# A fifth head pair whose softmax weights TensorE transposes in the banks of their own scores, with the first queries on another queue and a new list of schedule numbers

## The chip, the cores and the metric

One core of one Trainium2 chip runs the whole program. The metric is device time in microseconds of one launch, the median of several. A profile of one execution goes with it.

## The reference

Attention over a batch of 4, 8 heads, 576 tokens and 64 dimensions a head, then two feed-forward layers over the 2304 tokens, all in float32:

```python
scores = (q @ k.T) / sqrt(64)
scores = where(scores >= max(scores) - tau, scores, -1e9)      # tau = 0.02, by row
attn = exp(scores - max); attn = attn / (sum(attn) + 1e-9)
x = (attn @ v) as (2304, 512)
x = relu(x @ w1_in) ** 2 @ w1_out        # 512 -> 2048 -> 512
x = max(0.01 * h, h) @ w2_out            # h = x @ w2_in
```

## The kernel before

**Work and steps.** Heads are taken in pairs, so that there are 16 pairs (4 per batch element), numbered here from 0: the fifth pair is pair 4, the first of the second batch element. A pair has nine steps, each a block of 128 rows of scores: eight of 128 queries of one head, and one of the 64 remaining queries of both heads. A step multiplies queries and keys into two PSUM banks `s` (L498), takes the negated row maximum `nb` on VectorE (L508), the exponential `e` on ScalarE (L509), the threshold `th` and the masked product with its row sum on VectorE (L513), and the reciprocal `r` (L518). The ring `s` has two members, so step k+2 may write only when all that reads step k's banks is done.

**Two ways from there.** For pairs 0 to 3 (`nav=4`), `e` is scaled by `r` in float32 (L522 to L524), TensorE transposes it block by block into `pt` (L532, L533; two banks of a pool `ps_t` of their own, ring of one), ScalarE copies that into `PT`, and five float32 products with the values give an output chunk `o` (L598). For pairs 4 to 15 the weights are split into two float16 parts (`P16`; ScalarE L523 or another engine, and VectorE L554), a DMA transposes them into `PT` (L560), and fifteen float16 products give `o` (L594). Pairs 0 to 5 (`nat`) have float32 queries and keys, the later ones split them too. An output chunk leaves by ScalarE (`tmp`, L606), a sum into `xs` (ScalarE L608 and GpSimd L609, or VectorE L611) and a DMA into `x1d`.

**The feed-forward work.** Twelve of the 16 blocks of the first layer run for the first 1792 tokens in pieces (`h` L642, `y0`/`y1` L666) between the attention steps from the fifth pair on: their banks, `psf`, are opened when `ps_t` is closed, and their input is the first batch element's output. The rest of both layers (L775, L821) follows alone. Each weight block is read as float64 (`wraw`) and made into float32 and two parts by ScalarE and VectorE (L341 to L346), GpSimd and others; twelve blocks of the first layer are made beside the first pairs.

**Order.** Nothing is ordered by hand. `Plan.order` takes all operations with their priorities (`prio`, mostly the step number plus a number of `CFG`), models the time of each, and writes one fixed order per engine, choosing between engines by `price`. So each number of `CFG` can move any instruction. DMAs are issued by SyncE (SP), the first few by ScalarE's queue: `tau`, the first weight block's two halves, the first pair's queries, and `eye`.

Of the kernel before, what the change touches and what calls it, by code (L numbers as in the profile page):

```python
# [7 lines left out]
F32 = mybir.dt.float32  # L8
# [15 lines left out]

CFG = dict(
    price=[{'V': 4.8, 'A': 1.81, 'G': 1.1},
           {'V': 3.0, 'A': 0.84, 'G': 1.01},
           {'V': 2.82, 'A': 1.42, 'G': 1.25},
           {'V': 1.99, 'A': 1.06, 'G': 1.2},
           {'V': 3.0, 'A': 2.4, 'G': 1.5}],  # L30
    lead1=-2.0, xsg0=[0, 1, 2, 3], lbm=8, lb=[[0, 4], [0], [5], [0, 1, 2, 3, 5, 6]], xsm=4, xsg=[0, 3], dq=1.15,
    xu=False, pqk=-2.996, pd1=-0.75, pex=-1.791, pd2=0.3, ph=2.017, pl=1.4, hu=False, bg=2.008, lead=2.5, w0=22.155,
    wstep=2.3, fend=1.0, tol=0.2, hor=-0.021, xlead=5.801, nb=3, eb=3, pb=3, ptb=3, kvb=3, nat=(0, 1, 2, 3, 4, 5),
    nav=4, vb=2, tmb=1, gb=2, xb=1, w2step=2.57, wo=0.316, wrb=3, r1b=1, xrb=1,
)


# [208 lines left out]
def tile_kernel(ctx: ExitStack, tc: tile.TileContext, qT, kT, vv, w1, w2, tau, eye, out):  # L246
# [151 lines left out]
    def times(o, n):  # L398
# [1 line left out]
        return [("V", dve(n, True, True), lambda: nc.vector.tensor_scalar(out=o(), in0=o(), scalar1=qsc, scalar2=None, op0=ALU.mult), "K"),  # L400
                ("A", act(n, ap=True), lambda: nc.scalar.activation(o(), o(), AF.Copy, scale=qsc), "K"),
                ("G", pool1(n, True), lambda: nc.gpsimd.tensor_scalar(out=o(), in0=o(), scalar1=qsc, scalar2=1.0, op0=ALU.mult, op1=ALU.mult), "K")]
    order = [(b, p) for b in range(B) for p in range(NP)]
    steps = [(n, h, t) for n in range(len(order)) for h, t in
             [(0, 0), (0, 1), (1, 0), (1, 1), (0, 2), (0, 3), (None, MAIN), (1, 2), (1, 3)]]
    NS = len(steps)
    SPP = NS // len(order)
    SPB = SPP * NP

    def prep(n):  # L410
        b, p = order[n]
        o = pairs[n] = Box()
        h0 = 2 * p
# [46 lines left out]
        if n < CFG["nav"]:  # L460
# [15 lines left out]
    def step(i):  # L476
# [48 lines left out]
        if n < CFG["nav"]:  # L525

            op(scale(ev), [e, r_], [e], i + CFG["ph"], CFG["hu"])
            pt = val("ps_t", "pt", 1, [P, NH, P], F32)

            def flip():  # L530
                for j in range(MAIN):
                    nc.tensor.transpose(pt.get()[:, j], ev()[:, REM + j * P:REM + (j + 1) * P], eye_sb)  # L532
                nc.tensor.transpose(pt.get()[:, MAIN], ev()[:, 0:P], eye_sb)  # L533
            op(("T", NH * 0.109, flip), [e, eye_v], [pt], i + CFG["pl"], True)
            for dst, col, c0, c1 in ([(chunk(n, hh, 1), 2 * P, hh * REM, (hh + 1) * REM) for hh in range(2)] if h is None
                                     else [(chunk(n, h, t // 2), t % 2 * P, 0, P)]):
                op(rnd(lambda dst=dst, col=col, c0=c0, c1=c1: whole32(dst)[:, :, col:col + c1 - c0], lambda c0=c0, c1=c1: pt.get()[:, :, c0:c1], NH * (c1 - c0), True),
                   [pt], [dst], i + CFG["pl"], True)
# [33 lines left out]

    def values(key, i):
        n, h, c = key
        b, p = order[n]
        o = pairs[n]
        t0, w = spans[c]
        pt = chunks[key]
        pr = i + (CFG["lead1"] if n % NP == NP - 1 else CFG["lead"])
        ps = val("ps_o", "o", 1, [P, 512], F32)  # L580


# [24 lines left out]
        if key[0] % CFG["xsm"] in CFG["xsg0" if key[0] < NP else "xsg"]:  # L607
# [295 lines left out]
```

## Time and profile before

| | us |
|---|---|
| median of 3 runs | 1135.37 (1129.83 to 1136.39) |
| the profiled execution | 1133.95 |
| its span, first to last instruction | 1132.2 |
| TensorE busy in it | 1070.7 |
| VectorE / ScalarE / GpSimd busy | 689.3 / 544.4 / 596.4 |

The profile is of one execution. "Busy" is the union of an engine's recorded instructions; an idle time before an instruction is put down to what ended last before it started. The launch costs 1.75 us beside the span.

### The profile page before, as it was taken

What the parts mean: (1) busy time and instruction counts of PE and PEld (TensorE: products, weight loads), DVE (VectorE), ACT (ScalarE), POOL (GpSimd) and SP (SyncE); (2) the same over time, 40 slices, a digit from 0 to 9 for tenths busy, and PEclk for the clock granted to TensorE, in tenths of its full rate; (3) what the DMA queues carried; (4) which work ended last, traced back from release to release, by engine and by line L of the source; (5) the groups of instructions that cost most, each with busy time, mean ns of one, the idle gap of its engine ahead of it and who ended that gap; (6) DMA issues with size and microseconds to landing.
All of it is one profiled execution on the core that took longest, in us unless ns stands there. A gap on an engine that the chain in (4) does not pass through costs nothing.

```text
span 1132.2 us, 17792 instructions
## 1 busy us (share of the span) xinstructions
PE 1070.7 (95%) x6308; PEld 883.8 (78%) x6308; DVE 689.3 (61%) x1316; ACT 544.4 (48%) x978; POOL 596.4 (53%) x626
## 2 busy tenths in 40 slices
PE   5888799899999999999999999999999999999998
PEld 3544488688889988899888778878888888888887
DVE  4888998789878888864879985571312221211122
ACT  3887878778877788865434452231211111111121
POOL 3667678678776787654656664442322322232222
PEclk9999999999999999999999999999999999999999
DMA  5344578998998796865444365430010010010010
GB/s 151 104 133 119 147 164 174 180 163 171 176 160 166 148 169 116 152 107 174 151 153 131 112 199 173 158 121 1 28 48 1 1 56 1 1 38 1 0 39 19
DMA packets 197673, 121.83 MB, mean 108 GB/s; under 512 B 156752, under 2 KB 175312, under 8 KB 197584
## 3 DMA queue, kind: packets, MB, share of 16 engines
q1 hardware_dynamic: 196848, 119.28, 44.9%
q10 hardware_dynamic: 736, 1.41, 0.4%
q8 instruction: 50, 0.82, 0.3%
q14 instruction: 39, 0.32, 0.1%
HBM read 70.98 MB, written 17.83 MB: 78 GB/s over the span
## 4 chain that ended last, share of the span: by engine, by line
PE 71%; DVE 6%; DMA 5%; issue 3%; ACT 3%; POOL 2%; SPq 0%; POOLq 0%; DVEq 0%; ACTq 0%
PE y L821 23%; PE h L775 22%; PE y L666 8%; PE h L642 7%; PE o L594 5%; PE s L498 5%; DMA PT<-P 4%; DVE wraw L344 2%; DVE wraw L346 1%; ACT e L509 1%; DVE e L513 1%; DVE nb L508 1%; DVE wraw L342 1%; POOL gl L298 0%; PE o L598 0%
## 5 line engine op out<-in xcount | busy, mean ns | idle before, releaser
L298 POOL TENSOR_TENSOR gl<-r,gh 128x512 fp32r<-128x512 f32 (+1 forms) x140 | 182.0, 1301 | 323.6 <-DVE gh L287 272.8
L787 DVE TENSOR_TENSOR r<-h,r 128x512 f32<-128x512 f32 (+1 forms) x80 | 51.0, 638 | 280.5 <-ACT r L786 280.4
L786 ACT ACTIVATE r<-h 128x512 f32<-128x512 f32 (+1 forms) x80 | 44.5, 556 | 299.5 <-PE h L775 292.5
L498 PE MATMUL s<-KH,Q 128*128 128x288 f32 (+1 forms) x440 | 125.9, 381 | 16.6 <-DMA Q<-qT 10.4
L508 DVE TENSOR_REDUCE nb<-s 128x1 f32<-128x576 f32 x144 | 107.9, 750 | 39.7 <-PE s L498 38.9
L513 DVE SCALAR_TENSOR_TENSOR e<-s,th,e 128x576 f32<-128x576 f32 x144 | 116.2, 810 | 18.5 <-ACT e L509 15.3
L509 ACT ACTIVATE e<-s,nb 128x576 f32<-128x576 f32 x144 | 106.3, 739 | 21.7 <-DVE nb L508 15.6
L498 PEld LDWEIGHTS s<-KH,Q 128*128 128x128 f32 (+1 forms) x440 | 76.8, 190 | 37.5 <-issue 18.3
L554 DVE SCALAR_TENSOR_TENSOR P<-e,r,P 128x576 f16<-128x576 f32 x74 | 85.1, 1150 | 10.7 <-ACT P L523 10.4
L298 POOL TENSOR_TENSOR xl<-xr,xh 128x512 fp32r<-128x512 f32 (+1 forms) x49 | 65.6, 1347 | 30.4 <-ACT xh L285 24.3
L594 PE MATMUL o<-PT,VA 128*128 128x320 f16 (+1 forms) x432 | 63.3, 290 | 13.8 <-DMA PT<-P 10.8
L344 DVE SCALAR_TENSOR_TENSOR wraw<-wraw 128x512 int32<-128x512 int32 x64 | 68.5, 1070 | 8.5 <-ACT wraw L341 5.2
L346 DVE SCALAR_TENSOR_TENSOR wraw<-wraw 128x512 int32<-128x512 int32 x64 | 62.1, 970 | 1.1
L594 PEld LDWEIGHTS <-VA 128*128 128x128 bf16 x432 | 38.8, 99 | 28.7 <-issue 10.9
L285 ACT CAST gh<-r 128x512 fp32r<-128x512 f32 x67 | 41.2, 616 | 32.0 <-DVE r L784 22.6
L523 ACT ACTIVATE P<-e,r 128x576 f16<-128x576 f32 x60 | 46.2, 772 | 20.4 <-DVE r L518 8.9
L498 PE MATMUL s<-KL,Q 128*128 128x288 f32 x200 | 55.7, 294 | 0.0
L341 ACT ACTIVATE wraw<-wraw 128x512 f32<-128x512 f32 x64 | 43.7, 683 | 20.9 <-DMA wraw<-w 20.4
L342 DVE TENSOR_SCALAR wraw<-wraw 128x512 int32<-128x512 int32 x64 | 43.5, 683 | 13.6 <-DMA wraw<-w 13.6
L511 POOL TENSOR_SCALAR th<-nb,ca 128x1 f32<-128x1 f32 x73 | 31.3, 429 | 31.1 <-DVE nb L508 16.3
L609 POOL TENSOR_TENSOR xs<-xs,tmp 64x256 f32<-64x256 f32 (+1 forms) x40 | 36.0, 901 | 19.4 <-ACT xs L608 16.5
L287 DVE CAST gh<-r 128x512 fp32r<-128x512 f32 (+1 forms) x87 | 37.9, 437 | 8.7 <-PE y L821 0.6
(579 smaller groups left out, 3029.0 us busy)
## 6 DMA issues: line engine op xcount, KB each, us to landing
wraw<-w SPq DMA_DIRECT2D x62, 512.0 KB, 4.1
wraw<-qT SPq DMA_DIRECT2D x20, 288.0 KB, 4.1
wraw<-kT SPq DMA_DIRECT2D x20, 288.0 KB, 4.0
out<-yo SPq DMA_DIRECT2D x18, 256.0 KB, 2.1
VA<-vv SPq DMA_DIRECT2D x32, 128.0 KB, 3.1
x2d<-yo SPq DMA_DIRECT2D x16, 256.0 KB, 3.6
xr<-x2d SPq DMA_DIRECT2D x4, 1024.0 KB, 6.1
y1d<-ys SPq DMA_DIRECT2D x14, 256.0 KB, 2.5
```

The costliest lines, as they stand in the source:

```text
L298: alts.append(("G", pool2(n), lambda: nc.gpsimd.tensor_tensor(out=o(), in0=a(), in1=b(), op=alu), kind))
L344: op(("V", 0.9, lambda ui=ui, yi=yi: nc.vector.scalar_tensor_tensor(out=yi(), in0=ui(), scalar=3, in1=yi(), op0=ALU.logical_shift_left, op ...
L498: nc.tensor.matmul(ps.get()[r, g, 0:S2], lhsT=o.Q.get()[:, q], rhs=(kk.get() if o.KL else f32(kk.get()))[:, g_(g)], start=k == 0 or not o. ...
L508: op(("V", 0.75, lambda: nc.vector.tensor_reduce(out=nb.get(), in_=pv(), axis=AX.XY, op=ALU.max, negate=True)), [ps], [nb], i + CFG["pd1"] ...
L509: op(("A", 0.76, lambda: nc.scalar.activation(e.get(), pv(), AF.Exp, bias=nb.get(), scale=1.0)), [ps, nb], [e], i + CFG["pex"], True)
L513: op(("V", 0.89, lambda: nc.vector.scalar_tensor_tensor(out=e.get(), in0=pv(), scalar=th.get(), in1=e.get(), op0=ALU.is_ge, op1=ALU.mult, ...
L554: op(("V", dve2(S), lambda: nc.vector.scalar_tensor_tensor(out=lo(), in0=ev(), scalar=r_.get(), in1=hi(), op0=ALU.mult, op1=ALU.subtract)) ...
L594: nc.tensor.matmul(ps.get()[r, c_], lhsT=f_(v), rhs=parts16(pt)[:, j, c_], start=(k == 0), stop=k >= len(prods) - 2)
L642: nc.tensor.matmul(ps.get()[:, i], lhsT=a.get()[:, kc * P:(kc + 1) * P], rhs=x.get()[:, kc], start=(i == 0 and q == 0 and kc == 0), stop=( ...
L666: nc.tensor.matmul(yp[m // 2].get()[:, m % 2], lhsT=a.get()[:, c], rhs=x.get()[:, i], start=(f + i == 0 and q == 0 and m % 2 == 0), stop=( ...
L775: nc.tensor.matmul(ps.get()[:, 0:n], lhsT=a.get()[:, kc * P:(kc + 1) * P], rhs=x.get()[:, kc, 0:n], start=(q == 0 and kc == 0), stop=(q == ...
L821: nc.tensor.matmul(o(), lhsT=l, rhs=r, start=(first and q == 0), stop=(last and q == 2))
```

## The change

Pair 4 joins the first way (`nav=5`). No second bank pair is left for its transposes, since `psf` is opened at the same step as before, so they are written into the banks that held the step's own scores (`pt = ps if o.own`), in five blocks of 128 columns. Pair 4 keeps its nine steps, four output chunks and float32 products. The queries of the first pair are issued on SP's queue, right after the first keys, and no longer on ScalarE's; the zeros beside them are written by VectorE for head 0 and GpSimd for head 1. `two` is false, so its branch of the order of pairs does nothing. The list of numbers is another.

```diff
-    lead1=-2.0, xsg0=[0, 1, 2, 3], ..., lb=[[0, 4], [0], [5], [0, 1, 2, 3, 5, 6]],
+    lead1=1.04, xsg0=[1, 2, 3], ..., lb=[[0, 4], [0], [4, 5], [0, 1, 2, 3, 5, 6, 7]],
...
-    nav=4, vb=2, ..., wo=0.316,
+    nav=5, two=False, vb=2, ..., wo=1.444,
...
-                dma(lambda h=h: qs(h)[h * D:(h + 1) * D], lambda h=h: qT[b, h0 + h], [], [Q], at(0), D * S * 4, q=nc.sync if n else nc.scalar)
+                dma(lambda h=h, c0=c0, c1=c1: qs(h)[h * D:(h + 1) * D, c0:c1], lambda h=h, c0=c0, c1=c1: qT[b, h0 + h][:, c0:c1], [], [Q], at(0), D * (c1 - c0) * 4)
...
-            pt = val("ps_t", "pt", 1, [P, NH, P], F32)
+            pt = ps if o.own else val("ps_t", "pt", 1, [P, NH, P], F32)
+            pv_ = lambda: (pt.get().rearrange("p a b -> p (a b)")[:, 0:NH * P].rearrange("p (j q) -> p j q", j=NH) if o.own else pt.get())
...
-                    nc.tensor.transpose(pt.get()[:, j], ev()[:, REM + j * P:REM + (j + 1) * P], eye_sb)
+                    nc.tensor.transpose(pv_()[:, j], ev()[:, REM + j * P:REM + (j + 1) * P], eye_sb)
```

Where instructions moved is seen in the orders of both programs. First VectorE at the start: the second row that works on `wraw` begins the second half of the first weight block, and `nb<-s` is the first softmax maximum. Before:

```order
L342 TENSOR_SCALAR wraw<-wraw 128x512 [waits DMAHW2_49]
L344 SCALAR_TENSOR_TENSOR wraw<-wraw 128x512 [waits DVE_49,Activation_49]
L346 SCALAR_TENSOR_TENSOR wraw<-wraw 128x512 [waits DVE_49]
L342 TENSOR_SCALAR wraw<-wraw 128x512 [waits DMAHW7_49]
L508 TENSOR_REDUCE nb<-s 128x1 [waits PE_49]
```

Now (line numbers are higher by 8 to 14 in the changed file):

```order
L434 MEMSET Q_118 64x576
L342 TENSOR_SCALAR wraw<-wraw 128x512 [waits DMAHW2_49]
L344 SCALAR_TENSOR_TENSOR wraw<-wraw 128x512 [waits DVE_49,Activation_49]
L346 SCALAR_TENSOR_TENSOR wraw<-wraw 128x512 [waits DVE_49]
L342 TENSOR_SCALAR wraw<-wraw 128x512 [waits DMAHW5_49]
L519 TENSOR_REDUCE nb<-s 128x1 [waits PE_49]
```

The memset is new there; the maximum still stands behind the first operation on the second weight half, which waits for that half's DMA. Second, ScalarE at the first output chunk of pair 0. Before:

```order
L606 ACTIVATE tmp<-o 64x256
L608 ACTIVATE xs<-o 64x256
L509 ACTIVATE e<-s,nb 128x576
L285 COPY PT<-pt 128x5x128
L341 ACTIVATE wraw<-wraw 128x512
```

Now:

```order
L619 ACTIVATE tmp<-o 64x256
L520 ACTIVATE e<-s,nb 128x576
L285 COPY PT<-pt 128x5x128
L341 ACTIVATE wraw<-wraw 128x512
L285 COPY PT<-pt 128x5x128
```

`xs` has gone to VectorE, as at all four chunks of pair 0. Third, TensorE where the first batch element ends and the feed-forward pieces (`h`) begin; the numbered `s` are steps, in the order in which they were made. Before:

```order
L598 MATMUL o_1457<-PT_1372,VA_845 64x320 x5
L498 MATMUL s_1480<-KH_688,Q2_1000 128x288 x2
L642 MATMUL h_1508<-xh_1428,w0ih_140 128x256 x4
L498 MATMUL s_1517<-KH_688,Q2_1000 128x288 x2
```

Now:

```order
L611 MATMUL o_1426<-PT_1344,VA_833 64x320 x5
L509 MATMUL s_1446<-KH_688,Q2_1016 128x288 x2
L545 MATMUL s_1368<-eye_sb_75,e_1400 128x128 x4
L546 MATMUL s_1368<-eye_sb_75,e_1400 128x128
L655 MATMUL h_1469<-xh_1361,w0ih_140 128x256 x4
L509 MATMUL s_1479<-KH_688,Q2_1016 128x288 x2
L611 MATMUL o_1486<-PT_1436,VA_1150 64x256 x5
L655 MATMUL h_1469<-xl_1372,w0ih_140 128x256 x4
L655 MATMUL h_1469<-xh_1361,w0il_145 128x256 x4
L655 MATMUL h_1469<-xh_1361,w1ih_422 128x256 x4
L655 MATMUL h_1469<-xl_1372,w1ih_422 128x256 x4
L655 MATMUL h_1469<-xh_1361,w1il_430 128x256 x4
```

Each step of pair 4 now comes back as a transposition into its own `s`, with feed-forward pieces between. The first `h` follows step 40's scores before (`s_1480`) and step 38's now (`s_1446`).

## Rows read from the trace of the kernel before

**Rows 1.** The page: the span, and TensorE's busy time in it.
```profile
span 1132.2 us, 17792 instructions
PE 1070.7 (95%) x6308; PEld 883.8 (78%) x6308; DVE 689.3 (61%) x1316; ACT 544.4 (48%) x978; POOL 596.4 (53%) x626
```

**Rows 2.** Busy time by stage: stretch, its length, each engine, granted clock, DMA.
```profile
core 0: us, PE busy (x) PEld busy (x) DVE busy (x) ACT busy (x) POOL busy (x), PEclk, DMA share, GB/s
10.40:133.00 122.60, 101.54 (x517) 61.22 (x518) 100.66 (x240) 94.45 (x163) 79.62 (x116) 1.00 0.44 121
133.00:200.00 67.00, 60.11 (x438) 50.27 (x438) 60.75 (x115) 51.38 (x96) 52.28 (x55) 1.00 0.80 169
200.00:520.00 320.00, 305.45 (x2498) 273.80 (x2498) 251.00 (x571) 244.87 (x450) 231.59 (x270) 0.99 0.82 153
520.00:1132.00 612.00, 603.58 (x2856) 498.50 (x2856) 274.73 (x386) 151.74 (x269) 229.79 (x177) 1.00 0.23 73
```

**Rows 3.** TensorE's waits over the span: total us, times, longest.
```profile
PE pt L532 <- ACT PT L285: 11.3, 10, 1.8
PE s L498 <- DMA Q<-qT: 10.4, 1, 10.4
```

**Rows 4.** Timeline of the start: start, duration, instruction, idle time before it.
```profile
10.44 4.18 PE L498 MATMUL s<-KH,Q 128*128 128x288 f32 x8 [10.44 <-DMA Q<-qT]
...
12.52 0.43 DVE L342 TENSOR_SCALAR wraw<-wraw 128x512 int32<-128x512 int32 x1 [2.84 <-DMA wraw<-w]
12.86 0.75 DVE L508 TENSOR_REDUCE nb<-s 128x1 f32<-128x576 f32 x1
```

**Rows 5.** ScalarE's DMA queue from 3 to 10.5 us: packets, MB, share.
```profile
q10 hardware_dynamic: 459, 1.18, 49.4%
```

**Rows 6.** TensorE's timeline: a transposition before scores, and an output chunk in float32.
```profile
118.00 0.60 PE L532 MATMUL pt<-eye_sb,e 128*128 128x128 f32 x4
...
118.55 1.14 PE L498 MATMUL s<-KH,Q 128*128 128x288 f32 x4
...
130.96 1.98 PE L598 MATMUL o<-PT,VA 128*64 128x320 f32 x10
132.86 1.24 PE L498 MATMUL s<-KH,Q 128*128 128x288 f32 x4
```

**Rows 7.** An output chunk in float16 (timeline); 24 feed-forward products (the chain's pieces).
```profile
158.95 1.38 PE L594 MATMUL o<-PT,VA 128*128 128x320 f16 x9
...
160.73 0.74 PE L642 MATMUL h<-xh,w5il 128*128 128x256 f32 x4
...
172.14 2.83 PE y L666 x24
```

**Rows 8.** VectorE's split of the weights, 130 to 212 us: least, median, longest ns.
```profile
L554 DVE SCALAR_TENSOR_TENSOR P<-e,r,P x17: 794/1123/4553, 132.7 to 208.9; 128x576 f16<-128x576 f32 x17
```

**Rows 9.** TensorE's waits, windows 135 to 160, 180 to 200 and 200 to 210 us.
```profile
PE o L594 <- DMA PT<-P: 1.3, 2, 1.0
PE s L498 <- DVE e L513: 1.2, 1, 1.2
...
PE y L666 <- DVE gl L296: 1.3, 1, 1.3
...
PE o L594 <- DMA PT<-P: 2.7, 1, 2.7
PE o L594 <- DMA x1d<-xs: 1.2, 1, 1.2
```

**Rows 10.** ScalarE's output copies from 20 to 150 us: busy, mean ns, idle before.
```profile
L608 ACT ACTIVATE xs<-o 64x256 f32<-64x256 f32 (+1 forms) x18 | 7.2, 402 | 0.4
```

**Rows 11.** Timeline of one step of pair 4: its scores, and its masked product.
```profile
145.23 1.13 PE L498 MATMUL s<-KH,Q 128*128 128x288 f32 x4
...
151.41 4.55 DVE L554 SCALAR_TENSOR_TENSOR P<-e,r,P 128x576 f16<-128x576 f32 x1
...
155.95 0.80 DVE L513 SCALAR_TENSOR_TENSOR e<-s,th,e 128x576 f32<-128x576 f32 x1
```

More of the change, by code (lines that the diff above doesn't have):

```diff
@@ L26 @@
     price=[{'V': 4.8, 'A': 1.81, 'G': 1.1},
[L27 to L34, printed above, removed]
+           {'V': 3.0, 'A': 0.84, 'G': 0.86},
+           {'V': 2.79, 'A': 1.42, 'G': 1.47},
+           {'V': 2.26, 'A': 1.06, 'G': 1.2},
+           {'V': 2.68, 'A': 2.39, 'G': 1.5}],
+    lead1=1.04, xsg0=[1, 2, 3], lbm=8, lb=[[0, 4], [0], [4, 5], [0, 1, 2, 3, 5, 6, 7]], xsm=4, xsg=[0, 3], dq=1.15,
+    xu=False, pqk=-2.996, pd1=-0.399, pex=-1.791, pd2=0.3, ph=2.884, pl=1.4, hu=False, bg=2.008, lead=2.5, w0=22.155,
+    wstep=2.3, fend=1.0, tol=0.182, hor=-0.027, xlead=5.801, nb=3, eb=3, pb=3, ptb=3, kvb=3, nat=(0, 1, 2, 3, 4, 5),
+    nav=5, two=False, vb=2, tmb=1, gb=2, xb=1, w2step=2.57, wo=1.444, wrb=3, r1b=1, xrb=1,
 )
@@ L402, in times @@
                 ("G", pool1(n, True), lambda: nc.gpsimd.tensor_scalar(out=o(), in0=o(), scalar1=qsc, scalar2=1.0, op0=ALU.mult, op1=ALU.mult), "K")]
-    order = [(b, p) for b in range(B) for p in range(NP)]
-    steps = [(n, h, t) for n in range(len(order)) for h, t in
-             [(0, 0), (0, 1), (1, 0), (1, 1), (0, 2), (0, 3), (None, MAIN), (1, 2), (1, 3)]]
+    head, tail = [(0, 0), (0, 1), (1, 0), (1, 1)], [(0, 2), (0, 3), (None, MAIN), (1, 2), (1, 3)]
+    order = [(0, p, head) for p in range(NP)] + [(0, p, tail) for p in range(NP)] if CFG["two"] else [(0, p, head + tail) for p in range(NP)]
+    order += [(b, p, head + tail) for b in range(1, B) for p in range(NP)]
+    NAV = NP
+    steps = [(n, h, t) for n, (_, _, what) in enumerate(order) for h, t in what]
+    begin = [sum(len(w) for _, _, w in order[:n]) for n in range(len(order) + 1)]
+    last = {n for n in range(len(order)) if n + 1 == len(order) or (n + 1) % NP == 0}
     NS = len(steps)
-    SPP = NS // len(order)
-    SPB = SPP * NP
+    SPB = NS // B
     def prep(n):
-        b, p = order[n]
+        b, p, what = order[n]
         o = pairs[n] = Box()
+        o.b, o.nav, o.own, o.q = b, n < CFG["nav"], n >= NAV, [None] * 2
         h0 = 2 * p
@@ L417, in prep @@
         o.qs = qs = lambda h: Q.get()[:, h * QB:h * QB + S]
-        at = lambda k: (n - 1) * SPP - 1.5 + CFG["bg"] + k * SPP / 14 if n else -3.0 + k * 0.1
+        at = lambda k: begin[n - 1] - 1.5 + CFG["bg"] + k * len(order[n - 1][2]) / 14 if n else -3.0 + k * 0.1
         raw = lambda: val("stage", "wraw", CFG["wrb"], [P, 2 * S], F32)
@@ L424, in prep @@
             for h in range(2):
-                z = lambda h=h: qs(h)[(1 - h) * D:(2 - h) * D]
-                op([("V", dve(S), lambda z=z: nc.vector.memset(z(), 0.0)), ("G", dve(S), lambda z=z: nc.gpsimd.memset(z(), 0.0))], [], [Q], at(-1))
+                c0, c1 = (0, S) if len(what) > 5 else (0, 2 * P) if what is head and h == 0 else (REM, REM + 2 * P) if what is head else (2 * P, S) if h == 0 else (0, S)
+                z = lambda h=h, c0=c0, c1=c1: qs(h)[(1 - h) * D:(2 - h) * D, c0:c1]
+                zero = [("V", dve(c1 - c0), lambda z=z: nc.vector.memset(z(), 0.0)), ("G", dve(c1 - c0), lambda z=z: nc.gpsimd.memset(z(), 0.0))]
+                op(zero if n else zero[h], [], [Q], at(-1))
+                o.q[h] = c0, c1
             for h in range(2):
-                dma(lambda h=h: qs(h)[h * D:(h + 1) * D], lambda h=h: qT[b, h0 + h], [], [Q], at(0), D * S * 4, q=nc.sync if n else nc.scalar)
+                c0, c1 = o.q[h]
+                dma(lambda h=h, c0=c0, c1=c1: qs(h)[h * D:(h + 1) * D, c0:c1], lambda h=h, c0=c0, c1=c1: qT[b, h0 + h][:, c0:c1], [], [Q], at(0), D * (c1 - c0) * 4)
             dma(lambda: f32(kh.get()), lambda: kT[b, h0:h0 + 2].rearrange("h d s -> (h d) s"), [], [kh], at(0), 2 * D * S * 4)
@@ L459, in prep @@
         nv = NH * P
-        if n < CFG["nav"]:
+        if o.nav:
             return
@@ L574, in values @@
         n, h, c = key
-        b, p = order[n]
+        b, p, _ = order[n]
         o = pairs[n]
@@ L578, in values @@
         pt = chunks[key]
-        pr = i + (CFG["lead1"] if n % NP == NP - 1 else CFG["lead"])
+        pr = i + (CFG["lead1"] if n in last else CFG["lead"])
         ps = val("ps_o", "o", 1, [P, 512], F32)
@@ L598, in av32 @@
                 nc.tensor.matmul(ps.get()[(lo3, up3)[j % 2], 0:w], lhsT=o.VA.get()[0:rows, j, h, 0], rhs=whole32(pt)[0:rows, j, 0:w], start=j < 2, stop=j >= NH - 2)
-        if n < CFG["nav"]:
+        if o.nav:
             op(("T", 12 * mm(w) + 0.15, av32), [pt, o.VA], [ps], pr)
-        for k, z, passes in () if n < CFG["nav"] else ((0, NH, NH + 0.5), (NH, NH + MAIN, MAIN), (NH + MAIN, len(prods), 2.5)):
+        for k, z, passes in () if o.nav else ((0, NH, NH + 0.5), (NH, NH + MAIN, MAIN), (NH + MAIN, len(prods), 2.5)):
             op(("T", passes * mm(w) + 0.2 * (k == NH + MAIN), lambda k=k, z=z: av(k, z)), [pt, o.VA, o.VB], [ps], pr)
@@ L606, in values @@
         op(("A", act(w, True), lambda: nc.scalar.activation(tmp.get()[m, 0:w], ps.get()[l, 0:w], AF.Copy, scale=1.0 / UP)), [ps], [tmp], pr, CFG["xu"])
-        if key[0] % CFG["xsm"] in CFG["xsg0" if key[0] < NP else "xsg"]:
+        if key[0] % CFG["xsm"] in CFG["xsg0" if o.b == 0 else "xsg"]:
             op(("A", act(w, True), lambda: nc.scalar.activation(xs.get()[m, 0:w], ps.get()[m, 0:w], AF.Copy, scale=1.0 / UP)), [ps], [xs], pr, CFG["xu"])
@@ L680, in ffn @@
             dma(lambda m=m: y1d[j][2 * m * P:2 * (m + 1) * P, :].rearrange("(k p) t -> p k t", p=P), lambda ys=ys: ys.get(), [ys], [y1v[j]], pr, P * 2 * TA * 4)
-    avail = [SPB * ((j * TA + TA - 1) // S + 1) + CFG["xlead"] for j in range(NA)]
+    avail = [(SPB * ((j * TA + TA - 1) // S + 1) if j or not CFG["two"] else begin[NP]) + CFG["xlead"] for j in range(NA)]
     npieces = 5 * NFA // 2 + 2
@@ L698, in tile_kernel @@
     for i in range(NS):
-        if i == SPP * CFG["nav"]:
+        if i == begin[NAV]:
             def open1():
@@ L703, in tile_kernel @@
             oT = op(("N", 0.0, open1), [], [], i, after=[o for o in plan.ops if any(v.ring == "pt" for v in o.vals)])
-        if i % SPP == 0 and i // SPP + 1 < len(order):
-            prep(i // SPP + 1)
+        if i in begin and steps[i][0] + 1 < len(order):
+            prep(steps[i][0] + 1)
         step(i)
```

6 lines of the change are left out of this document (3 added, 3 removed).

## The prediction

> **What bounds the kernel now.** I read the page first: TensorE is busy 1070.7 of 1132.2 us [rows 1], so 61 us of idle time is all that any reordering can give back. The busy time by stage says where they lie [rows 2]. TensorE starts at 10.4 us [rows 4]. From there to 133 us, attention of the first batch element alone, it idles 122.6 - 101.5 = 21.1 us; from 133 to 200 us, pair 4 with the first feed-forward pieces, 67.0 - 60.1 = 6.9; from 200 to 520 us, 14.6; after it 8.4. From 133 us on TensorE is the bound, since the feed-forward pieces fill it, and every microsecond of TensorE work added there is paid unless an idle one goes. Before 133 us no engine is full: VectorE is busy 100.7 of 122.6 us and ScalarE 94.5, and the steps are held by the chain from engine to engine. TensorE's list of waits names the copy of the transposed weights on ScalarE first, 11.3 us in ten waits [rows 3]; the only larger single one is the 10.4 us for the first queries [rows 3]. The clock is at its upper level, 0.99 to 1.00 granted, in every stage [rows 2], so no stage has speed to win there.
>
> **The transposes.** Pair 4 gets nine of them, five blocks each. In front of other TensorE work one costs the distance to the next row: from 118.00 to 118.55 us, 0.55 us [rows 6]. Where nothing follows, the record of four of its blocks alone is 0.60, so five would be 0.75. That is 5.0 to 6.8 us for nine. I take 5.0, because feed-forward pieces stand behind them in the order. They lie on the path: pair 4 runs where TensorE is full.
>
> **The products.** An output chunk of 320 columns took 132.86 - 130.96 = 1.90 us in float32 [rows 6] and 160.73 - 158.95 = 1.78 in float16 [rows 7]. Four chunks at 0.12 are +0.5 us (0 to 0.5).
>
> **The first queries.** They leave ScalarE's queue, where the second weight half was issued behind the first of them, and go behind the first keys on SP's. The first scores can then start sooner. But the first maximum stands on VectorE behind an operation on that weight half, before as after: that operation started at 12.52 us, when the half had landed, and the maximum at 12.86 [rows 4]. So what counts is when the half lands. ScalarE's queue moved 1.18 MB in 7.5 us, 157 GB/s [rows 5]; without one head's 0.147 MB ahead of it, the half is there 0.147 / 157e-6 = 940 ns sooner. I take -0.9 us; the ends are 0 (SP's queue, now with more in front, takes the bandwidth) and -4.2 (the first scores' 4.18 us [rows 4], all done before the half lands). The memset that VectorE gets lies in its wait for weights and costs nothing; were that wait gone, it would cost one small operation, inside these ends.
>
> **The rest of the first stage.** ScalarE loses the four `xs` copies of pair 0, 0.40 us each [rows 10], and by the whole order two weight conversions less are placed before step 37. It is the engine that TensorE waits for most often there. VectorE gets the four sums, but nine thresholds go to GpSimd. I take -1.5 us, about a tenth of those waits; the ends are +1 (VectorE, the fuller of the two, is later) and -3.
>
> **What goes away in pair 4's stretch.** Waits on its DMA transposes, 1.3 us; one of 1.2 us for a masked product behind a split that took 4.55 us on VectorE instead of the median 1.12 [rows 8, 9, 11]; and 1.3 us for a feed-forward part that VectorE had late [rows 9]. Together -3.8 us (0 to -3.8). The nine splits leave VectorE, some 10 us at 1.12, but twelve more weight operations than before stand among pair 4's steps in the new order, so VectorE stays full there and no more than these waits is credited.
>
> **What comes in.** The scores' banks are held from the scores to the copy of their transposition, so step k+2 waits for step k's scaling, transposition and copy, where it waited for the masked product. Queued behind such a wait on TensorE are the feed-forward pieces, and with them everything later. The order leaves room: between step 38's scores and its transposition stand step 37's transposition, 24 feed-forward products, step 39's scores and one chunk. With 2.83 us for 24 products [rows 7], 1.1 for scores [rows 6] and 1.5 for a chunk of 256 columns (1.90 x 256 / 320), that is 1.1 + 0.55 + 2.8 + 1.1 + 1.5 = 7.0 us. A quiet chain is some 4 us, an estimate: maximum 0.75 [rows 4], mask 0.80 [rows 11], exponential and scaling over the same 576 columns about as much each, and small ones and signals between. A loaded one was longer: in the step that I show, 10.7 us from the scores to the mask, with the 4.55 us split in it [rows 11], so about 7 without that excess. I take +1.0 us for the nine steps; the ends are 0 and +12 (below). The Trainium skill's page "Perfetto Trace Analysis", section "Matmuls" under "Optimizing Tensor Performance", says that independent groups should rotate through different PSUM banks so that emptying one overlaps the next group; by it this reuse is the wrong way round. No row of before shows a transposition in the scores' banks.
>
> **Pair 5.** Its first chunks waited 2.7 us for a DMA transposition and 1.2 behind an output store [rows 9], with ten transfers of pair 4 ahead on the same queue. These are gone; I credit half, -2.0 us (0 to -3.9). After 210 us the order is new too, with the same work; I set 0, with 3 us either way.
>
> **Sum.** 5.0 + 0.5 - 0.9 - 1.5 - 3.8 + 1.0 - 2.0 + 0 = -1.7 us. The profiled execution took 1133.95 us, so 1132.3. The median of the runs is 1135.37, 1.4 above that execution, and the runs spread over 6.6; the forecast is for a run like the profiled one.
>
> **Rivals.** *The banks stall the steps (slower).* Place: steps 38 to 46 on TensorE. If the chain from scores to scaling takes over the 7.0 us that stands between, each step is late by the difference. For it: VectorE is busy 60.75 of 67 us there [rows 2], and the one loaded chain that I show was 10.7 us [rows 11]. Against it: the split that made that chain long is gone, and steps go in pairs, so that a late one has the next step's pieces too. At 1.2 us late for nine steps, +10.8 in place of +1.0: 1142. The skill's rule on rotating banks gives this side. It decides at 7.0 us: a shorter chain costs nothing.
>
> *VectorE's relief carries on (faster).* Without the splits, masks and feed-forward parts come on time; TensorE gets back all 6.9 us from 133 to 200 and half of the 14.6 after it [rows 2]. Then -6.9 - 7.3 + 5.5 - 2.4 = -11.1: 1123. For it: VectorE was busy at 91% from 133 to 200 us, against 78% from 200 to 520 [rows 2]. Against it: weight work moves into the place that is freed, and the waits after 200 us are split among causes that the change doesn't touch.
>
> *The change does not buy anything.* TensorE does 5.5 us more and the vanished waits come back under other names, as they do when one fixed order replaces another: 5.5 - 0.9 = +4.6, 1138.5.
>
> **Chances.** The forecast as summed, 1128 to 1137: 0.53. Bank stalls around 1142, reaching 1148: 0.20. Relief around 1123: 0.15. Nothing bought, around 1138.5: 0.12. A range of 1123 to 1143 leaves out half of the stalls' 0.20 and half of the relief's 0.15, under 0.2. Of the unknown costs it holds each alone, and not all at their bad ends at once (+23). One per cent of the time, about what a measurement of this kernel can tell from no change, is 11.3 us. Faster by that needs the relief to reach below 1122.6: 0.10. Slower needs stalls beyond 1145: 0.12. Within it 0.78.
>
> **What would show each step.** Transposes: nine more groups, 0.55 us apart from their follower, and TensorE busy 5 to 6 us more. Queries: first scores at 6 to 7 us, the first maximum at about 11.9. First stage: the first feed-forward product 1 to 4 us sooner. Vanished waits: none on DMA transposes before 180 us. Banks: TensorE's waits for the copy of a transposition, in front of scores, small from 133 to 200 us; 5 us or more of them would make the forecast wrong, as would an idle time in 200 to 520 us that differs from 14.6 by more than 5.

## The result, and the profile of the changed kernel

The changed kernel took 1118.69 us in the median of four runs (1117.47 to 1121.41), against 1133.62 for the kernel before on the same chip: a ratio of 0.987, interval 0.984 to 0.991. It is about 15 us faster. The forecast was 1132.3, the range ended at 1123, and "faster by over 1%" had a chance of 0.10: the prediction was wrong. One execution of e7 below took 1199.55 us at a granted clock of 0.847 and is left out. The page of the profiled execution (1117.47 us), the two rows that answer to [rows 1]:

```profile
span 1115.7 us, 17813 instructions
PE 1069.9 (96%) x6333; PEld 883.8 (79%) x6333; DVE 694.9 (62%) x1339; ACT 533.8 (48%) x957; POOL 585.3 (52%) x618
```

Busy time by stage, answering to [rows 2] (same columns), cut at about the same places of the work:

```profile
7.50:121.00 113.50, 98.34 (x519) 59.08 (x520) 99.09 (x226) 91.14 (x158) 76.61 (x116) 1.00 0.48 132
121.00:195.00 74.00, 71.92 (x513) 59.05 (x512) 61.69 (x125) 60.60 (x109) 61.43 (x70) 1.00 0.64 148
195.00:505.00 310.00, 296.92 (x2441) 266.88 (x2439) 248.25 (x568) 240.03 (x444) 227.21 (x255) 1.00 0.84 151
505.00:1115.00 610.00, 602.67 (x2867) 498.74 (x2865) 284.35 (x417) 140.02 (x246) 217.50 (x170) 1.00 0.23 74
```

Length less TensorE's busy time is its idle time. The account by TensorE, against the terms of the sum:

| us | before | after | change | forecast |
|---|---|---|---|---|
| TensorE starts | 10.4 | 7.5 | -2.9 | -0.9 (with the maximum) |
| idle, first stage | 21.1 | 15.2 | -5.9 | -1.5 |
| idle, pair 4's stretch | 6.9 | 2.1 | -4.8 | -3.8 + 1.0 |
| idle, to the end of attention | 14.6 | 13.1 | -1.5 | -2.0 |
| idle, last stage | 8.4 | 7.3 | -1.1 | 0 |
| busy | 1070.7 | 1069.9 | -0.8 | +5.5 |

These sum to -17.0, and the span became 16.5 us shorter. Idle time fell in every stage. The nine transpositions of pair 4 took 4.8 us of TensorE's time, and still it was no busier in all; why is said below. Both columns are of one execution each, and the changed kernel's is the fastest of its four. The start, answering to [rows 4] (start, duration, instruction, idle before it):

```profile
7.51 4.18 PE L509 MATMUL s<-KH,Q 128*128 128x288 f32 x8 [7.51 <-DMA Q<-qT]
...
9.75 1.35 DVE L342 TENSOR_SCALAR wraw<-wraw 128x512 int32<-128x512 int32 x1 [0.99 <-DMA wraw<-w]
...
11.03 0.75 DVE L519 TENSOR_REDUCE nb<-s 128x1 f32<-128x576 f32 x1
```

TensorE's waits in pair 4's stretch, 121 to 195 us (total, times, longest), first rows:

```profile
PE o L607 <- DMA PT<-P: 1.1, 1, 1.1
PE y L679 <- POOL gl L298: 0.5, 1, 0.5
PE h L655 <- ACT xh L285: 0.2, 1, 0.2
```

No product of scores there waits for the copy of a transposition, so holding the banks shows no cost on TensorE. The chains on DMA transpositions, masked products and VectorE's feed-forward parts of [rows 9] are gone but for 1.1 us. Last, VectorE's wait for scores in the first stage, before (12.5 to 133 us) and after (11 to 121):

```profile
DVE nb L508 <- PE s L498: 13.2, 20, 1.8
```

```profile
DVE nb L519 <- PE s L509: 6.1, 14, 0.9
```

### The profile page after: what moved, and what is told of

Its sections match the earlier page's. It is cut to its first block, busy times and chain, and to the rows that moved or that the text cites. A ratio compares the mean times of both kernels' runs of the same rounds, so it can differ in the third digit from the quotient of the medians.

```text
span 1115.7 us, 17813 instructions
## 1 busy us (share of the span) xinstructions
PE 1069.9 (96%) x6333; PEld 883.8 (79%) x6333; DVE 694.9 (62%) x1339; ACT 533.8 (48%) x957; POOL 585.3 (52%) x618
## 4 chain that ended last, share of the span: by engine, by line
PE 50%; DVE 6%; issue 2%; ACT 1%; DMA 1%; POOL 0%; SPq 0%; POOLq 0%; DVEq 0%; ACTq 0%
PE y L835 22%; PE h L789 21%; PE y L679 3%; PE h L655 2%; DVE wraw L344 2%; DVE wraw L346 1%; PE o L607 1%; DVE wraw L342 1%; DMA PT<-P 1%; DVE r L798 1%; PE s L509 1%; POOL P L298 0%; DVE gl L296 0%; SPq L573 0%; DMA y1d<-ys 0%
## 5 line engine op out<-in xcount | busy, mean ns | idle before, releaser
L509 PE MATMUL s<-KH,Q 128*128 128x288 f32 (+1 forms) x440 | 124.9, 379 | 14.6 <-DMA Q<-qT 7.5
L298 POOL TENSOR_TENSOR xl<-xr,xh 128x512 fp32r<-128x512 f32 (+1 forms) x46 | 58.9, 1287 | 33.8 <-DVE xh L287 26.2
L344 DVE SCALAR_TENSOR_TENSOR wraw<-wraw 128x512 int32<-128x512 int32 x64 | 63.2, 987 | 6.3 <-ACT wraw L341 3.3
L567 DVE SCALAR_TENSOR_TENSOR P<-e,r,P 128x576 f16<-128x576 f32 x57 | 64.3, 1129 | 1.2 <-ACT P L534 1.0
L607 PE MATMUL o<-PT,VA 128*128 128x320 f16 (+1 forms) x396 | 56.6, 287 | 8.3 <-DMA PT<-P 7.4
L346 DVE SCALAR_TENSOR_TENSOR wraw<-wraw 128x512 int32<-128x512 int32 x64 | 58.6, 915 | 1.1
L342 DVE TENSOR_SCALAR wraw<-wraw 128x512 int32<-128x512 int32 x64 | 45.9, 718 | 11.0 <-DMA wraw<-w 11.0
L287 DVE CAST gh<-r 128x512 fp32r<-128x512 f32 (+1 forms) x93 | 42.6, 458 | 15.8 <-PE y L835 7.7
L607 PEld LDWEIGHTS <-VA 128*128 128x128 bf16 x396 | 35.2, 98 | 20.5 <-DMA PT<-P 5.7
L285 ACT CAST gh<-r 128x512 fp32r<-128x512 f32 (+1 forms) x61 | 37.3, 611 | 27.4 <-DVE r L798 18.8
L298 POOL TENSOR_TENSOR P<-e,P 128x576 f16<-128x576 f32 x32 | 42.8, 1339 | 12.4 <-ACT P L285 7.6
L534 ACT ACTIVATE e<-e,r 128x576 f32<-128x576 f32 x54 | 41.5, 772 | 4.7 <-DVE r L529 4.6
```

The lines of the kernel that those rows point to most:

```text
L298: alts.append(("G", pool2(n), lambda: nc.gpsimd.tensor_tensor(out=o(), in0=a(), in1=b(), op=alu), kind))
L342: op(("V", 0.7, lambda yi=yi: nc.vector.tensor_scalar(out=yi(), in0=yi(), scalar1=29, scalar2=None, op0=ALU.logical_shift_right)), [raw], ...
L344: op(("V", 0.9, lambda ui=ui, yi=yi: nc.vector.scalar_tensor_tensor(out=yi(), in0=ui(), scalar=3, in1=yi(), op0=ALU.logical_shift_left, op ...
L346: op(("V", 0.9, lambda ui=ui, yi=yi: nc.vector.scalar_tensor_tensor(out=yi(), in0=ui(), scalar=-(1 << 31), in1=yi(), op0=ALU.bitwise_and, ...
L509: nc.tensor.matmul(ps.get()[r, g, 0:S2], lhsT=o.Q.get()[:, q], rhs=(kk.get() if o.KL else f32(kk.get()))[:, g_(g)], start=k == 0 or not o. ...
L567: op(("V", dve2(S), lambda: nc.vector.scalar_tensor_tensor(out=lo(), in0=ev(), scalar=r_.get(), in1=hi(), op0=ALU.mult, op1=ALU.subtract)) ...
```

## The experiments

The expectations name their theories by letters; what each run decides stands in words behind it. In one table: the fifth and the 37th maximum (the 37th is the first of pair 4's steps; timeline of VectorE), the first feed-forward product, the last attention maximum (all of the profiled execution), the median, its ratio to before on the same chip, the mean granted clock of its runs, and what the falls below 1 cost at most, (1 - clock) x time.

| kernel | 5th | 37th | first `h` | last | median | ratio (interval) | clock | at most |
|---|---|---|---|---|---|---|---|---|
| before | 26.35 | 121.35 | 133.7 | 499.8 | 1132.43 | | 0.9947 | 6.0 |
| after | 20.82 | 110.09 | 121.3 | 486.7 | 1118.69 | 0.987 (0.984, 0.991) | 0.9982 | 2.0 |
| e1 queue only | 20.89 | 115.58 | 129.4 | 499.0 | 1132.64 | 1.000 (0.999, 1.002) | 0.9947 | 6.0 |
| e2 pair only | 22.69 | 117.38 | 130.8 | 506.6 | 1136.44 | 1.004 (1.002, 1.006) | 0.9940 | 6.8 |
| e3 numbers only | 23.64 | 112.93 | 126.8 | 502.9 | 1134.72 | 1.001 (0.999, 1.003) | 0.992 | 9 |
| e4 after, old queue | 24.42 | 113.65 | 124.9 | 496.8 | 1120.58 | 0.991 (0.988, 0.994) | 0.9984 | 1.8 |
| e5 after, pair 4 the old way | 21.12 | 110.33 | 128.1 | 503.3 | 1133.32 | 1.002 (1.000, 1.005) | 0.9883 | 13.3 |
| e7 xsg0 only | 22.97 | 113.43 | 140.0 | 498.4 | 1134.07 | 1.001 (0.999, 1.004) | 0.991 | 10 |
| e8 due times only | 22.88 | 110.91 | 135.4 | 502.3 | 1134.41 | 1.002 (0.999, 1.004) | 0.990 | 11 |
| e13 xsg0 and due times | 22.00 | 111.15 | 134.7 | 501.2 | 1135.64 | 1.005 (1.003, 1.007) | 0.9916 | 9.5 |
| e9 after, DMAs back | 20.79 | 109.85 | 121.1 | 492.9 | 1122.32 | 0.991 (0.987, 0.994) | 0.9974 | 2.9 |
| e10 after, VectorE's work back | 21.41 | 110.55 | 121.8 | 498.7 | 1127.80 | 0.998 (0.996, 1.001) | 0.9959 | 4.6 |

The row of before is of the 26 runs beside e5; beside e10 to e13 its median was 1130.62, beside the changed kernel 1133.62. Ratios are to the runs on the same chip; medians from different chips are not quite comparable, since before itself differs by 3 us between them. The first four columns are of one execution each; that of e4 took 1127.44 us, 7 above its median. The last column holds only if every fall of the clock lies where TensorE is the bound.

**The parts one by one (e1 to e4).** The queue alone, in the kernel before, with every engine's order as it was:

```diff
-dma(..., D * S * 4, q=nc.sync if n else nc.scalar)
+dma(..., D * S * 4, q=nc.sync)
```

> The kernel before with one edit: the first pair's queries go on SP's queue behind the first keys; the order of every engine's computing instructions is the same as before. Theory A (the queue is worth what the first maximum gains, 1.8 us between the two profiles): about 1.8 us faster than before, 0.998. Theory B (the whole lead that the changed kernel has at its seventh maximum, 5.6 us, comes from the start): about 5.6 us faster, 0.995. Theory C (of the forecast: the second weight half holds the maximum): 0.9 us, within the spread.

The pair alone: the changed file with the old list and queue, and pair 4 the new way.

```diff
-    lead1=1.04, xsg0=[1, 2, 3], ..., nav=5, ..., wo=1.444,
+    lead1=-2.0, xsg0=[0, 1, 2, 3], ..., nav=5, ..., wo=0.316,
```

> The kernel before with pair 4 transposed by TensorE in its scores' banks, old numbers and old queue. The planner makes a new order. Theory A (pair 4's way is worth the idle time that went from 133 to 200 us, 5.2 us, and TensorE's nine transposes cost 5.0): about as before, 0.996 to 1.003. Theory B (VectorE's relief is the gain): 8 to 12 us faster, 0.990 or less. Theory C (banks held stall the steps): slower, 1.005 or more.

The numbers alone: the new list with `nav=4` and the old queue.

> The changed kernel's numbers with pair 4 on the old way and the queries on the old queue. Theory A (most of the gain is the first batch element's 36 steps in an order that leaves less idle time, and that comes from the numbers): 6 to 10 us faster than before, 0.991 to 0.995. Theory B (the numbers are worth nothing without the pair they were chosen for): as before or slower, 0.999 to 1.01.

And the change without its queue part:

> The changed kernel with the first pair's queries back on ScalarE's queue; the order of every engine's computing instructions is that of the changed kernel. Theory A: 1.8 us slower than the changed kernel, 1120.5, 0.989 of before. Theory B: 5.6 us slower than it, 1124, 0.992.

None of the three parts gains alone, so no theory of one cause stands. The pair and the numbers together gain (e4, 0.991), and the queue adds a little (after, 0.987). Yet each part alone is 4 to 8 us ahead of before at the 37th maximum, and none is at the end of attention.

Those leads are not all the parts' own. The profile of before has the latest fifth maximum of all, 26.35 us. e1 is 5.5 us ahead there, and e2 3.7, though e2 leaves the queue as it was. From the fifth to the 37th maximum e1 and e2 take 94.7 us, as before does (95.0), and every kernel with the whole new list takes 89.1 to 89.3. So the list shortens that stretch by 5.7 us, and what stands ahead of it depends on the queue and on the clock of the one execution that was profiled. The scores of steps 2 and 3, and of 4 and 5, in TensorE's timeline, before and changed kernel:

```profile
16.98 4.18 PE L498 MATMUL s<-KH,Q 128*128 128x288 f32 x8 [2.35 <-DVE e L513]
...
24.19 3.20 PE L498 MATMUL s<-KH,Q 128*128 128x288 f32 x8
```

```profile
13.87 3.78 PE L509 MATMUL s<-KH,Q 128*128 128x288 f32 x8 [2.19 <-issue]
...
19.65 2.13 PE L509 MATMUL s<-KH,Q 128*128 128x288 f32 x8
```

The same eight instructions take 4.18 us at TensorE's lower level (1.2 GHz) and 2.13 at its upper (2.4 GHz). The upper is there for good from 26.4 us in before and from 17.1 in the changed kernel. The clock column of [rows 2] says 1.00 even so, because these two profiles hold no record of the clock before. The queue alone doesn't set these times: of the kernels with the old queue, e4 gets there at 24.5 us too, but e2, e3, e7, e8, e11 and e13 between 18.1 and 21.5.

The 16.5 us by which the changed kernel's span is shorter are then 5.5 up to the fifth maximum, 5.7 from there to the 37th, 1.9 to the last and 3.4 behind it. In e1, whose order is that of before, the lead of the start is lost behind the 37th maximum. TensorE's waits for DMA transpositions from 195 to 505 us show where some of it went, before and e1:

```profile
PE o L594 <- DMA PT<-P: 9.5, 8, 2.7
```

```profile
PE o L594 <- DMA PT<-P: 12.0, 10, 2.8
```

**The pair's way, in the new order (e5, e9, e10).** e5 is the changed kernel with `nav=4`:

> The changed kernel without its first part: pair 4 goes the old way, with the new numbers and the queries on SP's queue. Additive theory (each lead at the first feed-forward product is kept to the end): the first such product at 122.7 us, 4.2 sooner than with the numbers alone, and 1130.5 us in all. Theory F (without the pair's change a lead is eaten by longer waits and the clock's falls after them): the first product as early, but 1132 to 1136 in all.

It is as early as the changed kernel at the 37th maximum, and 17 us later at the last, so the additive theory (1130.5 us) fails and F's time (1132 to 1136) holds, though not its first product. Its waits between 121 and 200 us:

```profile
PE s L509 <- DVE e L524: 6.1, 5, 3.4
```

Scores wait there for masked products on VectorE, where pair 4's splits are back. Its clock was the lowest of all, 0.988. Two experiments put back one load each in the changed kernel, as work that nobody reads. First ten DMA transpositions:

```diff
-            op(("T", NH * 0.109, flip), ...)
+            fl = op(("T", NH * 0.109, flip), ...)
+            if o.own: fl.extra = back     # nc.sync.dma_start_transpose of e into P16
```

> The changed kernel with the ten DMA transposes of pair 4 put back as extra work whose result nobody reads: after each of its steps the scaled weights, as 2-byte words, are transposed into the float16 buffers that stand empty until pair 5. The order of all five engines' other instructions is that of the changed kernel. Theory D (the DMA queue paces the stretch after 133 us, and a lead is kept only since these ten transfers are gone): most of the changed kernel's gain is lost, 1126 or more. Theory E (their DMA time had been hidden; the order of TensorE's work and fewer gaps give the gain): within 2 us of the changed kernel, 1117 to 1121.

It took 3.6 us more than the changed kernel, by the medians, between what D and E expect. But the two intervals overlap, and e4, which has no added transfer, has the same ratio: a price of these transfers isn't shown. Its profile does show one way in which they could cost. ScalarE waits for a weight block, the exponential and the copy that empties a score bank stand behind that, and TensorE's scores wait for the copy (ScalarE, then TensorE):

```profile
156.38 0.68 ACT L341 ACTIVATE wraw<-wraw 128x512 f32<-128x512 f32 x1 [2.94 <-DMA wraw<-w]
156.94 0.74 ACT L520 ACTIVATE e<-s,nb 128x576 f32<-128x576 f32 x1
157.57 0.69 ACT L285 COPY PT<-s 128x640 f32<-128x640 f32 x1
```

```profile
158.31 2.29 PE L509 MATMUL s<-KH,Q 128*128 128x288 f32 x4 [2.51 <-ACT PT L285]
```

In the changed kernel that block didn't hold ScalarE up, and there is no such wait. Then nine products on VectorE:

```diff
+                    nc.vector.scalar_tensor_tensor(out=P16s[i % 3][:, 0:S], in0=ev(), scalar=r_.get(), in1=ev(), op0=ALU.mult, op1=ALU.subtract)
```

> The changed kernel, with nine products on VectorE put back as extra work: after each of pair 4's transpositions VectorE makes, from the scaled weights, a float16 tile that nobody reads, in the shape of the split that the kernel before had there (1.12 us at the median, some 10 us in all). All engines' other instructions keep their order. Theory V (VectorE's relief is what lets the changed kernel go on without waits from 130 to 200 us): TensorE's waits for VectorE's masked products and feed-forward parts come back, 5 to 10 us, and clock falls behind them; 1125 to 1132. Theory N (it is the order as a whole, not VectorE's ten microseconds): idle time within 2 us of the changed kernel's, 1119 to 1121.

It took 1127.8, 9 us more than the changed kernel, and the two intervals lie apart (by the ratios to before, 0.998 against 0.987, it is 12 to 13): theory V holds in size, and a clock fall of 6.83 us goes with the longest wait. The added work was more than meant, as VectorE's row from 121 to 200 us shows (eight of the nine):

```profile
L550 DVE SCALAR_TENSOR_TENSOR P<-e,r 128x576 f16<-128x576 f32 x8 | 11.8, 1478 | 0.8 <-ACT e L534 0.8
```

All nine took 12.6 us and not 10. And the wait was not where V put it: it stood on the banks that the scores share. TensorE's waits in the same stretch, and the longest in the timeline:

```profile
PE s L509 <- ACT PT L285: 3.6, 2, 3.0
...
PE s L509 <- DVE e L524: 0.5, 1, 0.5
```

```profile
145.46 0.63 PE L659 MATMUL h<-xh,w4il 128*128 128x256 f32 x4
149.08 0.85 PE L509 MATMUL s<-KH,Q 128*128 128x288 f32 x1 [2.99 <-ACT PT L285]
```

So the rival's stall is there when the chain from scores to copy is late, by VectorE's load here and by a late weight block in e9. In the changed kernel it is absent.

**The first stage (e7, e8, e13).** Which numbers make it shorter? In the kernel before, `xsg0` alone, the due times alone, and both:

```diff
-xsg0=[0, 1, 2, 3]   pd1=-0.75    ph=2.017
+xsg0=[1, 2, 3]      pd1=-0.399   ph=2.884
```

> The kernel before with one number changed, the one that takes the four xs copies of pair 0 from ScalarE and GpSimd and gives the sums to VectorE. The planner makes a new order. Of the 6.8 us by which the new numbers bring the first feed-forward product forward, theory G (ScalarE, which TensorE waits for, is relieved) gives this number 3 us or more: first product at 131 or sooner. The forecast gave it about 1 us: 132 to 133.5. Time in all 1129 to 1134 by either.

> The kernel before with two numbers changed: the maximum's priority is later by 0.35 of a step, the scaling's by 0.87. New order. Theory H (the due times hold the first 36 steps' order together): the first feed-forward product 3 us or more sooner, at 131 or less. Theory G: not moved by more than 1.5 us. Time in all 1130 to 1137 by either.

> The kernel before with two of the new list's numbers together: the first pair's output sums on VectorE (xsg0 without 0), and the due times of the maximum and of the scaling (pd1, ph). Each alone gave no earlier first feed-forward product (139.9 and 135.3 us against 133.7). Theory I (the two together make the shorter first stage): the product at 127 to 129 us, as with the whole list (126.9), and the time within 0.5% of before, since the later stages lose it again. Rival J (the prices or lead1 are needed too): the product at 132 us or later.

By the first feed-forward product all three look worse than before (140.0, 135.4 and 134.7 us against 133.7), and theories G, H and I, as they were put, fall. But that was the wrong place to read, since the order decides which step the product follows. At the 37th maximum e8 is 10.4 us ahead of before, and e7 7.9. Some 3.4 us of each are there at the fifth maximum already; from there on the due times alone give 7.0 us, `xsg0` alone 4.5 and both 5.8, where the whole list gives 5.7. VectorE's rows of the 37th, of before and of e8:

```profile
121.35 0.74 DVE L508 TENSOR_REDUCE nb<-s 128x1 f32<-128x576 f32 x1
```

```profile
110.91 0.75 DVE L508 TENSOR_REDUCE nb<-s 128x1 f32<-128x576 f32 x1
```

So the shorter first stage is to be had in many ways, and it is worth nothing by itself: in e8 the last maximum is 2.5 us later than before.

**The clock (e11, e12).** In the profile of before, TensorE's clock fell twice to its lower level (1.2 GHz, granted share one half) for 3.41 us, at 200.5 and 565.7 us, each time after it had stood idle, 2.73 and 1.79 us. The first (windows, columns as in [rows 2]):

```profile
198.00:200.50 2.50, 0.06 (x1) 0.00 (x0) 2.01 (x7) 2.50 (x4) 1.15 (x3) 1.00 0.86 183
200.50:204.00 3.50, 3.21 (x15) 1.55 (x15) 1.62 (x4) 0.77 (x2) 3.09 (x3) 0.52 1.23 193
```

In the changed kernel's profile there is none between 17 us and the very end; after its longest idle time of the later stages the clock stayed up:

```profile
216.80:219.00 2.20, 0.08 (x1) 0.09 (x2) 2.20 (x8) 1.07 (x3) 2.20 (x2) 1.00 1.00 124
219.00:222.40 3.40, 3.40 (x29) 2.72 (x30) 0.60 (x5) 1.05 (x2) 3.17 (x3) 1.00 0.58 111
```

Theory K says that the idle times make the falls. e12 makes three of them in the changed kernel, in front of output chunks (`rest` is a small tile of its own):

```diff
+            if k0 == 0 and key in ((7, 0, 1), (10, 0, 1), (13, 0, 1)):
+                nc.tensor.matmul(ps.get()[:, 0:P], lhsT=eye_sb, rhs=eye_sb, ...)
+                nc.scalar.copy(rest, ps.get()[:, 0:P])
+                for _ in range(8): nc.scalar.copy(rest, rest)
+                nc.tensor.matmul(ps.get()[:, 0:P], lhsT=eye_sb, rhs=rest, ...)
```

> The changed kernel, with TensorE made to stand idle in front of three output chunks (second chunks of pairs 7, 10 and 13): it waits there for nine copies in a row on ScalarE, about 2.5 us. Theory K: a clock fall of 3.41 us follows at least two of the three idle times, the mean granted clock goes from 0.998 to about 0.994, and each costs its 2.5 us and 1.7 more, 10 to 13 us in all: 1129 to 1132. Rival L: no more falls than the changed kernel had, and only the idle times, 5 to 8 us: 1124 to 1127.

The time was 1131.51, 12.8 us more than the changed kernel's, the clock 0.9928, and in the profile a fall began within 0.5 us of the end of each of the three idle times of 2.99 us. The first of them:

```profile
252.38 0.69 PE L611 MATMUL o<-rest,eye_sb 128*128 128x128 f32 x2 [2.99 <-ACT rest L610]
```

```profile
249.60:252.70 3.10, 0.33 (x2) 0.33 (x3) 0.43 (x2) 2.85 (x10) 0.00 (x0) 0.97 0.66 138
252.70:256.30 3.60, 3.60 (x18) 1.84 (x18) 2.69 (x6) 1.58 (x4) 0.19 (x1) 0.55 0.02 5
256.30:262.00 5.70, 5.39 (x44) 5.16 (x43) 4.19 (x5) 3.75 (x9) 4.54 (x4) 1.00 0.39 76
```

K holds for these three: 9.0 us of idle time and three falls of 1.7 are 14.1, and 12.8 showed by the medians (some 15 by the ratios to before, 1.001 against 0.987). It is no rule for each single idle time: in e13 two of 2.34 and 2.43 us, at 191 and 395 us, had no fall behind them, and in e3 the clock fell at 284.3 us with no idle time of over 1.0 us in the 12 us before. e11 is the reverse, on e2:

```diff
+    FILL = {(6, 0, 0): 10, (6, 0, 1): 18, (8, 0, 1): 14, (13, 0, 0): 17}
+            if k0 == 0:
+                for _ in range(FILL.get(key, 0)):
+                    nc.tensor.matmul(ps.get()[:, 0:P], lhsT=eye_sb, rhs=eye_sb, start=True, stop=True)
```

> The kernel with the pair part alone, in which TensorE waited 1.4, 2.3, 1.8 and 2.2 us for transposed weights in front of four output chunks, and the granted clock fell for 3.41 us after three of these. In front of the same four chunks TensorE now multiplies the unit matrix by itself, 10, 18, 14 and 17 times, into the bank that the chunk then overwrites; it is no useful work. Theory K (the clock falls because TensorE stood idle): the falls near 229, 294 and 437 us are gone, the mean granted clock goes from 0.994 to about 0.998, and the time is 4 to 5 us less than without the added products, about 1131.5. Rival L (the falls come with the load, or at random): as many falls, clock 0.994, 1136 to 1138.

The profile had no fall before its end (clock 1.0), but the mean over four runs was 0.996, and the time 1141.83 (ratio 1.010, 1.006 to 1.014), slower than e2. The filling was mis-sized: each product is two instructions, and the 18 took 4.18 us in front of a wait of 2.3:

```profile
224.76 4.18 PE L610 MATMUL o<-eye_sb 128*128 128x128 f32 x36
```

At 0.116 us for one, all 118 are 13.7 us, for 7.7 of waits. And three of the four runs had a clock of 0.994 to 0.996, within the 0.992 to 0.997 of e2's. So e11 decides nothing; e12 carries K.

## Why the prediction was wrong

Two steps failed. One is the clock: the prediction left it out of the sum, since "no stage has speed to win there", and less time at the lower level took some 6 us from TensorE's busy time, which was forecast at +5.5 us and came out at -0.8. The other is the first stage: the terms of -0.9 and -1.5 us stood for 2.9 us of earlier start and 5.9 us of idle time that went. Beside that, the sum added its terms as if each lasted to the end, and the parts run alone show that they don't.

**Transposes and products: right by themselves.** Pair 4's nine transpositions took 0.46 to 0.71 us each, 4.8 in all; 5.0 was forecast. But the consequence "TensorE busy 5 to 6 us more" failed, 0.8 us less. Of that difference of 6.3 us, the two clock falls that are gone are 3.4, and the scores, transpositions and chunks of the first four pairs took 2.7 us less, as the lower level of the start ended 9 us sooner.

**Clock: the step that was left out.** "No stage has speed to win there" rested on the mean clock of whole stages [rows 2], where two falls show as 0.99 and the slow start not at all. The start was to be read from [rows 4], 4.18 us for eight products of scores, against 1.14 for four later [rows 6]. By the mean clock of all runs the falls took at most 6.0 us before and 2.0 after: about 4 of the 15 us. Of before, the five runs at a clock of 0.999 or 1.0 took 1125.0 to 1127.8; the changed kernel's two at 1.0 took 1117.5 and 1118.2, so that some 9 us remain at an equal clock. The Trainium skill's page "Perfetto Trace Analysis", section "Matmul Optimizations", says that the engine scales its power with its use, so that products should run back to back in batches; e12 agrees as far as the clock goes, at 1.7 us for each fall.

**First queries: under-sized.** -0.9 forecast, -1.8 at the first maximum; the first scores came at 7.5 us and not at 6 to 7. The half weight block landed 2.8 us sooner (9.75 against 12.52), not 0.94; the operation on it then took 1.35 us and not 0.43. That the lead is 5.5 us at the fifth maximum was not in the sum: 2.9 of it are the earlier start of TensorE, and 2.6 go with the sooner end of its lower level, which isn't shown to be the queue's doing. But by e1 alone the queue is worth nothing at the end, and beside pair and numbers 1.9 us (e4), within the two kernels' spread.

**The rest of the first stage: under-sized.** "About a tenth of those waits" was a guess from the copies of `xs` alone. VectorE's wait for scores halved, 13.2 to 6.1 us, its stage had 5.9 us less TensorE idle time, and the first feed-forward product came 12.4 us sooner and not 1 to 4. From the fifth to the 37th maximum the list gives 5.7 us. The copies of `xs` alone are worth 4.5 of such a gain (e7), and the due times, to which the sum gave no term, are enough for all of it (e8).

**What goes away, and pair 5: near in size.** -4.8 net against -2.8 in pair 4's stretch, -1.5 against -2.0 behind it.

**Banks: right here, with a thin margin.** +1.0 forecast, nothing measured. The rival's mechanism is real: with 1.4 us more on VectorE for each step, e10 has a bank stall of 3.0 us. With the rule of the Trainium skill's page "Perfetto Trace Analysis", section "Matmuls", that groups should rotate through banks, the changed kernel's trace doesn't agree, and e10's does: it depends on how late the chain is that empties them.

**The rival that was nearest.** "VectorE's relief carries on" gave 1123, with its price of 11 us and 0.15 chance. Its mechanism is supported in the new order: taking VectorE's relief away cost 9 us or more (e10), though by a stall on the banks. What the DMAs' relief is worth (e9) isn't shown. It is not enough by itself: e2 has the relief with the old numbers and is slower than before: after 195 us it still waits 9.9 us for DMA transpositions (before 9.5) and 3.1 for masked products, with three clock falls. What failed in the sum is its form. It added parts, each by its own waits. The parts don't add: queue, pair and numbers alone give 0.0, +0.4 and +0.1%, all together -1.3%. From 121 us TensorE is the bound, so a lead of the steps counts only if its work starts earlier and it then doesn't wait; and a longer wait there can lower the clock for a while behind it (e12). e5 shows both: a lead of 11.0 us at the 37th maximum, none of pair 4's transpositions on TensorE, and yet 6.1 us of waits for masked products and up to 11.3 us more of clock falls than the changed kernel.

**Still open.** Why the numbers and the pair fit each other, beyond the VectorE load in pair 4's stretch, isn't settled: the new list came together with the pair's new way, and every other mixture gives an order of its own. Which of the remaining numbers (prices, `lead1`, `wo`, the tolerances) matter after 121 us wasn't tried.

## What to carry to other kernels

Where one engine is the bound, make the account by that engine (start, idle by stage, busy, clock) and not by adding vanished waits; a lead ahead of that stage is worth only what arrives as earlier work of the engine without new waits. Price an idle time of TensorE of some 2 to 3 us in a busy stage with the clock fall that may follow it, look for falls in narrow windows, since a stage's mean hides them, and read the start's clock from the length of equal products. Compare two profiles from a common point on, since the first steps of one execution can lie 5 us apart from those of another. Test an edit's parts in the order they were planned for: alone, each of these three looked worthless.

## What was not expected of the hardware

The clock's falls lasted 3.41 us (6.83 or 10.24 in some). In before each of the two came after an idle time of TensorE of 1.8 us or more and in e12 after 2.99, while one of 2.12 us in the changed kernel and one of 2.43 in e13 had none. At the start TensorE stayed at its lower level until 26.4 us in the profile of before, 16 us after its first product. One of VectorE's operations of the start took 1.35 us (9.75 to 11.10) in place of 0.43 on the same shape; GpSimd worked from 9.53 to 10.82 us beside it, and stood idle in before.
